# Batch 1's time shift mix goes to VectorE, wv is loaded in four pieces, five more zero matmuls and new orders

## The chip, the cores and the metric

The kernel runs on one core of one Trainium2 chip. The metric is the device time of one execution in microseconds (us). The engines are TensorE (PE in the profile, PEld for its weight loads), VectorE (DVE), ScalarE (ACT), GpSimd (POOL) and SyncE (SP); the last two issue most of the transfers, and ScalarE a few.

## The reference

Two layers, the second fed by the first. Everything comes and goes in float32.

```python
# attention, 8 batches x 8 heads, 576 positions, 64 wide
q_s = softmax(q, axis=-1)
k_s = softmax(k, axis=2)                       # over the positions
kv  = einsum('bhsd,bhse->bhde', k_s, v)
x   = einsum('bhsd,bhde->bhse', q_s, kv)       # then laid out as (8, 576, 512)
# channel mix
x_prev = x shifted by one position, zeros first
xk = mu_k * x + (1 - mu_k) * x_prev            # 512 wide
xr = mu_r * x + (1 - mu_r) * x_prev
k  = relu(xk @ w_k)                            # 512 x 1024
v  = (k * k) @ w_v                             # 1024 x 512
out = sigmoid(xr @ w_r) * v                    # w_r is 512 x 512
```

## The kernel before, in words

**Two halves of the work.** The attention goes by pairs (b, g): batch b, and g is 0 or 1 for half of the heads. The channel mix goes by ten units of up to 512 positions (`UNITS`, two halves of four batches each); a unit covers positions of one or two batches.

**Names.** Every step is an operation with a name, put on one engine (function `graph`). ORDER is a long string of those names, and it alone sets in which sequence each engine gets its steps; a number behind a colon is the buffer that the step takes. An engine works strictly through its own list, so a step that waits holds up everything behind it on that engine. For pair bg:

- `load{bg}{q,k,v}{n}` fetches the raw tiles (batches 0 and 1 in two parts of 288 KB, later ones as one of 576 KB), L204; `expq`, `expk` (L328) and `cast` for v (L334) are ScalarE's; `rsum`, `rrec`, `scale` normalise q on VectorE (L343, L347, L352).
- `TKV{bg}` is one block on TensorE: it turns q (L367) and forms k-softmax times v (L397). `rz` and `w` (L404, L414) bring the result back on VectorE as the small matrix of the attention, `qt` (L375) copies the turned q back on ScalarE.
- `X{bg}` forms x. Where the mix is **not folded** (batches 2 to 7) it is one block of 8 matmuls (L537), done inside the next pair's block, then called `B{bg}`, or alone for the pairs in ALONE. ScalarE copies x out (`xs`, `xb`, L543 and L546), and VectorE makes the mix: `edge`, `diff` (x minus shifted x, L555), four `sc` (times mu, L560), and two `mix` (plus shifted x, L565), `mix{bg}0` for xk and `mix{bg}1` for xr.
- Where it is **folded** (FUSED: batches 0 and 1) the small matrix is first multiplied by mu and by 1 - mu (`kvn`, L414 for batch 1; `wp{bg}0` on VectorE and `wp{bg}1`, for batch 1 on GpSimd, L475). Then `X{bg}0` and `X{bg}1` give xk and xr straight from TensorE, 16 matmuls each (L487), and `x{bg}{m}0` (ScalarE) and `x{bg}{m}1` (VectorE) copy them out (L497).

A unit i has `k{i}{f}` (eight, L621; a trailing .2 is the second half of one that was split by g), `relu{i}{f}` on ScalarE (L608), `sq{i}{f}` on VectorE (L612), `r{i}{m}` with w_r (L653), `th{i}{m}` on ScalarE (L658), `v{i}{m}{h}` with w_v (L673, h counts its parts), `o{i}{m}` on VectorE (L679) and `st` for the store. In unit 0 a v goes in as many parts as w_v has pieces, and a part waits for its piece alone; in the other units it has two parts.

**The ramp.** The q and k of batch 0 come through the queues of SP and ScalarE. Everything else is issued by GpSimd in the order that ORDER gives: v of batch 0, the weights `wk00`, `wk01`, `wk10`, `wk11` (quarters of w_k, tiles wk_aa to wk_bb), `wr`, `wv0` to `wv2`, `muload` (mu, that only the unfolded mix needs) and batches 1 to 7. At most eight of GpSimd's transfers are under way: the ninth issue waits until the first has landed, and so on. That makes GpSimd's own waits a record of landings. `k` steps that need g=0 alone want wk_aa, their .2 parts wk_ab; `k04` to `k07` want both wk_ba and wk_bb. Before there is real work, TensorE does matmuls on a tile of zeros (`fill`, L294), 22 of them.

Of the kernel before, what the change touches and what calls it, by code (L numbers as in the profile page):

```python
# [44 lines left out]
ACT!load00q0:0 zero ident load00q1 ACT!load00k0:1 load01q1:2 ACT!load01q0 rows load00v consts warm  # L45
load00k1 load01v late load01k0:3 load10q0:4 wk00 wk01 expq001:0 expq000 load11q0:5 rsum001:0
ACT!load01k1 rsum000 load10k0:6 expq011:1 rrec001 wk11 rrec000 rsum011:1 fill:1 fill.2:2 fill.3:3
fill.4:0 fill.5:1 fill.6:2 fill.7:3 fill.8:0 fill.9:1 fill.10:2 fill.11:3 fill.12:0 fill.13:1
fill.14:2 fill.15:3 fill.16:0 wide:0 scale000:0 expq010 expk000:0 rsum010 expk001 scale001
widecopy wk10 rrec010 fill.17:1 fill.18:2 KV001:0 rrec011 scale010:1 KV000 T00:1 rest Z00 qt00:0  # L50
scale011 rz00:0 expk010:1 fill.19:3 fill.20:1 fill.21:1 T01:3 edge00 kvn00:0 load10q1 expk011
fill.22:1 KV010:2 wp000:0 expq100:2 wr wp001 X000:1.0 qt01:1 KV011 x0001 Z01 load10k1 x0000 rz01:1
X001:0.3 kvn01:1 wp010:1 k02:0 x0010 edge01 k00:1 x0011 X010:1.0 load11q1 k03:2 x0100 x0101 k01:3
wv0 rsum100:2 k00.2 expk100:2 load10v1:7 k02.2 wp011 expq110:0 k03.2 relu00:0 k01.2 load10v0
X011:0.1 relu01:1 k07:1 sq01:0 load11v0:8 sq00 expq101 k05:3 load11v1 relu02:2 rsum101 relu03:1
k06:0 rrec100 sq02 relu05:0 sq03 x0110 k04:2 x0111 relu06:2 sq05 load11k1:9 r00:3 relu07:1
# [6 lines left out]
X110:1.0 mucopy k13:3 load30v0:8 x1101 x1100 k11:0 wp101 o01 expq210:2 k13.2 rsum200:0 k11.2
load31k0:9 relu13:1 X111:0.1 relu11:0 load40q0:10 k12:2 x1111 x1110 k17:3 o03 expk200:1 load30k0:0
sq11:1 k10:0 st03.2 sq13 k16:1 st00 expq300:0 rrec200 rsum210:1 load40v0:2 st03 X101:1.0 st01
relu17:2 k12.2 x1011 st00.2 x1010 k10.2 load31v0:3 sq17 relu16:0 k14:3 scale200:1 relu10:1
relu12:2 r12:1 cast210:0 sq10 load60q0:1 TKV20:0 rsum300:2 relu14:1 r11:0 th12:4 rrec210 rrec300
load41q0:4 rz20:1 expk210:2 k15:2 sq12 w20:0 scale210:2 r10:3 qt20:1 v120:1 sq16 relu15:2
scale300:0 expq310:1 B21:1.0 load50q0:5 sq14 th10:5 v110:2 rz21:2 sq15 xs20:0 xb20 w21:1
load40k0:7 rsum310:3 v100:3 qt21:0 v121 edge20 diff20:0 th11:6 v111 cast300:1 sc2000:0 X21:0.1  # L70
sc2011:1 o11 r13:0 xs21:1 load41k0:8 xb21 sc2010 o12 v101 expk300:0 edge21 rrec310 r20:2 diff21:1
expk310:1 load41v0:0 sc2001 v130:1 sc2101:2 mix200 th20:1 load60v0:9 TKV30:1 sc2100 th13:0
sc2111:0 mix210 v131 cast310:2 sc2110 k27:2 cast400:0 o13 load51q0:3 rz30:0 k21:0 scale310:1
st13.2 relu27:0 load50k0:2 st13 expq400:2 k22:1 o10 k20:2 w30:2 relu22:1 load71v0:10 st10 mix201
qt30:2 st11 k23:3 sq27:0 st11.2 rsum400:0 relu21:2 k24:1 st01.2 relu23:0 st10.2 B31:0.1 mix211
expk400:2 sq23 k26:0 rz31:1 relu24:0 rrec400 load50v0:7 sq21 xb30:0 w31:0 k25:3 sq24 scale400:2
relu20:2 r22:1 xs30 qt31:1 sq20 r23:2 edge30 diff30:0 relu25:0 B40:1.0 relu26:2 sq22 sc3001:2
expq410:0 v200:3 sc3000 mix300 th22:0 v220:0 load71k0:4 rz40:2 sq25 th23:6 rsum410:1 xs31:1 r21:1
xb31 v230:2 sq26 expq500:1 edge31 sc3011:1 v201 diff31:1 cast410:1 load61q0:5 w40:1 v231 sc3101:0
sc3100 th21:3 rrec410 load61k0:0 mix310 v221 expq510:2 o23 r30:1 o20 qt40:0 load71q0:3 k33:2  # L80
# [6 lines left out]
rrec600 st23.2 sc4001:0 th33:2 scale510:2 v331 expq610:1 k46:3 sc4000 qt51:0 relu43:0 o33
load60k0:5 B50:1.0 relu46:1 cast510:0 scale600:0 k47:2 st23 k42:0 cast600:1 v300:3 load70k0:1 sq46
qt60:2 sq44 rz50:1 mix400 v311 relu47:1 xs41:1 xb41 v320:2 o31 relu42:2 sq47 v301 expq700:2 st31.2
edge41 sq42 diff41:1 st21 r41:1 st21.2 expk510:2 o30 v321 sc4101:1 st30.2 sc4100 sq43 st31 k45:0  # L90
sc4110:2 mix410 st30 r40:3 relu45:1 expk600:0 o32 v410:0 sq45 rsum610:1 th41:6 k50:2 sc4111 k52:1
relu50:2 w50:0 rsum700:2 cast610:2 v411 k51:2 relu52:0 o41 mix411 k53:1 relu51:1 rrec610 B51:0.1
# [18 lines left out]
relu81:2 st73.2 sq80:0 k83:2 sq81 relu82:0 k84:1 sq82 relu83:1 k85:0 sq83 relu84:2 k86:3 sq84
relu85:0 k87:2 sq85 relu86:1 r80:1 sq86 relu87:2 r81:0 sq87 th80:5 v800:3 th81:4 v810:2 v801 v811
o80 r82:1 st80 o81 st80.2 r83:0 th82:6 st81 st81.2 v820:3 th83:0 v830:2 v821 v831 o82 k90:1 st82
o83 k91:0 st82.2 relu90:0 k92:3 st83 relu91:1 sq90:1 k93:2 relu92:2 sq91 st83.2 k94:1 relu93:0
sq92 k95:0 relu94:1 sq93 k96:3 relu95:2 sq94 k97:2 relu96:0 sq95 r90:1 relu97:1 sq96 sq97 r91:0
th90:3 v900:3 th91:2 v901 v910:2 o90 v911 st90.2 st90 v910.2:1 o91 v911.2 st91.2 st91 o91.2 st91.3
# [734 lines left out]
```

## Time and profile before

The three timed executions took 195.57, 195.60 and 195.91 us, median 195.6. The profiled execution took 195.56 us; its span, from the first to the last instruction, is 193.8 us, so 1.8 us lie around it.

| what | profiled execution |
|---|---|
| its time, and its span | 195.56 us, 193.8 us |
| granted TensorE clock, mean | 0.997 |
| VectorE busy | 149.7 us, 77% |
| ScalarE busy | 140.8 us, 73% |
| last matmul ends, read from TensorE's timeline | 190.1 us |

To read it: busy shares are means over a ramp, a long middle and an end that have different limits. The timeline of an engine lists its instructions with their start, what they took and, in brackets, how long the engine stood before them and who ended that.

### The profile page before, as it was taken

To read this page: it belongs to the slowest core of one execution; us is meant where nothing else is said; L and a number is where in the kernel's file an instruction comes from. 1 tells how busy PE (TensorE), PEld (TensorE's weight loads), DVE (VectorE), ACT (ScalarE), POOL (GpSimd) and SP (SyncE) were. 2 spreads that over 40 slices of the span, in tenths; PEclk is the share of its full clock that TensorE was granted. 3 is DMA by queue.
4 is the path that set the end of the run, shared out by engine and by line. 5 is a ranking of instruction groups with operands and counts; after the bars stand their busy time and mean duration, and the time that the engine had idled before them with its cause. 6 is when DMAs were issued, how large, how long until landed. Compare 5 with 4: busy or idle time off the path is not lost.

```text
span 193.8 us, 4763 instructions
## 1 busy us (share of the span) xinstructions
PE 186.3 (96%) x1873; PEld 90.4 (47%) x1873; DVE 149.7 (77%) x347; ACT 140.8 (73%) x218; POOL 43.5 (22%) x70
## 2 busy tenths in 40 slices
PE   7789999999999999999999999999999999999992
PEld 2264445435444554554555444444444444444751
DVE  1977668699999999999989998999925469622532
ACT  3777899899999999989996798767325732652340
POOL 8444347794324212341110000000000000000000
PEclk9999999999999999999999999999999999999998
DMA  6999999999999999899799604787334122403413
GB/s 198 315 267 292 268 347 303 401 390 392 414 391 391 392 408 355 258 331 351 169 220 113 223 4 96 156 207 150 70 71 92 57 50 58 112 0 80 96 42 108
DMA packets 23586, 41.86 MB, mean 216 GB/s; under 512 B 9344, under 2 KB 12684, under 8 KB 23564
## 3 DMA queue, kind: packets, MB, share of 16 engines
q0 software_dynamic: 9440, 27.99, 46.1%
q1 hardware_dynamic: 13308, 12.13, 24.8%
q10 hardware_dynamic: 816, 1.44, 2.1%
...
## 4 chain that ended last, share of the span: by engine, by line
PE 81%; DMA 12%; POOL 3%; ACT 2%; issue 0%; DVE 0%; POOLq 0%
PE mm_c L673 11%; PE mm_d L673 10%; PE mm_c L621 8%; PE mm_a L621 7%; PE mm_b L621 7%; PE mm_b L653 7%; PE mm_d L621 7%; DMA wk_bb<-in_moe_w_k_dram 7%; PE mm_a L673 6%; DMA raw_h<-in_v_dram 5%; PE mm_b L673 5%; PE mm_a L653 4%; PE mm_d L653 3%; PE mm_c L653 1%; PE att_b L397 1%; PE att_a L537 1%
## 5 line engine op out<-in xcount | busy, mean ns | idle before, releaser
L673 PEld LDWEIGHTS <-k_a 128*128 128x128 bf16 x144 | 13.8, 98 | 16.7 <-issue 0.5
L653 PEld LDWEIGHTS <-xr 128*128 128x128 bf16 x144 | 13.9, 98 | 16.2 <-issue 0.2
L673 PEld LDWEIGHTS <-k_b 128*128 128x128 bf16 x152 | 14.4, 98 | 15.0 <-issue 0.2
L653 PE MATMUL mm_b<-wr,xr 128*128 128x512 bf16 x64 | 16.4, 379 | 0.0
L621 PEld LDWEIGHTS <-wk_ab 128*128 128x128 bf16 x80 | 7.6, 98 | 8.2 <-issue 0.8
L621 PEld LDWEIGHTS <-wk_bb 128*128 128x128 bf16 x80 | 7.8, 98 | 7.7
L621 PEld LDWEIGHTS <-wk_aa 128*128 128x128 bf16 x80 | 7.4, 98 | 8.2 <-issue 0.9
L621 PEld LDWEIGHTS <-wk_ba 128*128 128x128 bf16 x80 | 7.5, 98 | 7.8 <-issue 0.2
L653 PE MATMUL mm_a<-wr,xr 128*128 128x512 bf16 x36 | 9.3, 380 | 0.0
L673 PE MATMUL mm_c<-wv_a,k_a 128*128 128x512 bf16 x32 | 8.2, 379 | 0.0
L608 ACT ACTIVATE rel_b<-mm_b 128x512 bf16<-128x512 f32 (+1 forms) x7 | 4.0, 571 | 4.9 <-PE mm_b L621 4.8
L608 ACT ACTIVATE rel_a<-mm_b 128x512 bf16<-128x512 f32 (+1 forms) x8 | 4.6, 572 | 4.0 <-PE mm_b L621 3.6
L621 PE MATMUL mm_c<-xk,wk_aa 128*128 128x512 bf16 (+1 forms) x26 | 7.3, 363 | 0.0
L621 PE MATMUL mm_c<-xk,wk_ab 128*128 128x512 bf16 (+1 forms) x26 | 7.3, 363 | 0.0
L612 DVE TENSOR_TENSOR k_a<-rel_b 128x512 bf16<-128x512 bf16 (+1 forms) x14 | 5.3, 380 | 2.5 <-ACT rel_b L608 2.5
L673 PE MATMUL mm_d<-wv_a,k_b 128*128 128x512 bf16 x28 | 7.2, 379 | 0.0
L653 PE MATMUL mm_d<-wr,xr 128*128 128x512 bf16 x28 | 7.2, 379 | 0.0
L612 DVE TENSOR_TENSOR k_b<-rel_a 128x512 bf16<-128x512 bf16 (+1 forms) x14 | 5.5, 390 | 1.8 <-ACT rel_a L608 1.3
L608 ACT ACTIVATE rel_c<-mm_a 128x512 bf16<-128x512 f32 (+1 forms) x11 | 6.0, 549 | 0.7 <-PE mm_a L621 0.7
L612 DVE TENSOR_TENSOR k_b<-rel_b 128x512 bf16<-128x512 bf16 (+1 forms) x14 | 5.5, 390 | 1.3 <-ACT rel_b L608 0.9
L612 DVE TENSOR_TENSOR k_b<-rel_c 128x512 bf16<-128x512 bf16 (+1 forms) x12 | 4.7, 391 | 1.9 <-ACT rel_c L608 1.6
L621 PE MATMUL mm_d<-xk,wk_ba 128*128 128x512 bf16 (+1 forms) x22 | 6.1, 360 | 0.0
(352 smaller groups left out, 534.0 us busy)
## 6 DMA issues: line engine op xcount, KB each, us to landing
...
```

The costliest lines, as they stand in the source:

```text
L397: kn.nc.tensor.matmul(kn.half(slot, r)[two[u], KVO:KVO + n], lhsT=kn.eks[ek.index][two[r], j, u, :], rhs=by, start=(j == 0), stop=(j == J ...
L537: kn.nc.tensor.matmul(kn.half(slot, u)[two[r], to:to + n], lhsT=kn.ws[w.index][two[u], r, :], rhs=x_columns(r, u, at, n), start=True, stop ...
L608: kn.nc.scalar.activation(out=kn.rels[rel.index][:, 0:n], in_=kn.bank(kf)[:, 0:n], func=ACT.Relu, scale=HALF_ROOT)
L612: kn.nc.vector.tensor_tensor(out=kn.k2s[k2.index][:, fc, 0:n], in0=kn.rels[rel.index][:, 0:n], in1=kn.rels[rel.index][:, 0:n], op=ALU.mult)
L621: kn.nc.tensor.matmul(kn.bank(kf)[:, 0:n], lhsT=kn.wk[fc // 4][ct % 2][:, ct // 2, (fc % 4) * 128: (fc % 4) * 128 + 128], rhs=kn.xs[0][:, ...
L653: kn.nc.tensor.matmul(kn.bank(rps), lhsT=kn.xs[1][:, ct, c:c + 128], rhs=kn.wr[:, ct, :], start=(ct == 0), stop=(ct == CT - 1))
L673: kn.nc.tensor.matmul(kn.bank(vps)[:, 0:width], lhsT=kn.k2s[k2.index][:, ft, 128 * m:128 * m + 128], rhs=wv_of(ft)[:, part], start=(ft == ...
```

## The change

- FUSED names pairs now and holds only those of batch 0. So for batch 1 `kvn`, `wp`, the four folded X blocks and the eight `x` copies go. Pair (1, 0)'s X is done inside (1, 1)'s block, which is now called `B11`; `X11` is alone; each pair has `w`, `xs`, `xb`, `edge`, `diff`, four `sc` and two `mix`.
- w_v comes in four pieces of two row tiles each rather than in three of 4, 2 and 2; unit 0's v steps have four parts.
- `muload` goes from GpSimd's queue to SP's, behind SP's loads of batch 0.
- FILLS goes from 22 to 27; the five are placed behind `fill.18`, right before `KV001`, the first real block.
- ORDER is new throughout. (Below, q100 is `load10q0`, the first part of pair (1, 0)'s q, and so on.) In GpSimd's queue the q, k and v of batch 1 go ahead of wv, and partly of the other weights. Behind batch 0's v it was q100, wk00, wk01, q110, k100, wk11, wk10, q101, wr, k101, q111, wv0, v101, v100, v110, v111, k111, k110, wv1, wv2, v20, mu. It is wk00, q110, q101, q100, wk01, q111, wk11, wk10, k101, v101, k100, v100, wr, v111, k111, k110, v110, wv0, wv1, wv2, wv3, q21, v20. On TensorE `TKV10` is ahead of unit 0's r steps, `B11` behind them and ahead of all of unit 0's v steps, and half of unit 4's k steps go in front of and between unit 3's. VectorE and ScalarE follow.

```diff
-WV = (0, 4, 6, 8)
+WV = (0, 2, 4, 6, 8)
-FILLS = 22
+FILLS = 27
-FUSED = (0, 1)
+FUSED = ((0, 0), (0, 1))
-ALONE = ((2, 1), (B - 1, 1))
+ALONE = ((1, 1), (2, 1), (B - 1, 1))
...
-th02:2 scale101:2 v020:3 wv2 scale100 cast101:0 v030:1 load20v0:10 rrec111 cast100 scale111:0
-muload v000:0 th01:3 rsum110 cast110:1 v010:2 load20q0:0 rrec110 cast111 scale110 TKV10:0
+relu06:0 load11v0 k05:3 relu05:2 wv0 wv1 rrec111 scale111:0 TKV10:0 sq07 wv2 rz10:2 r01:0
+relu04:1 r03:2 r02:3 w10:0 r00:1 qt10:2 cast111:1 expk111:0 wv3 expk110 cast110 sq04 load21q0:10
+scale110 th01:0 B11:1.0 th00:1 v010:0 rz11:0 sq05 load20v0:0 sq06 th03:2 v030:1 v000:2 xb10:0
+xs10 w11:1 edge10 v001 qt11:0 v031 v011 diff10:0 sc1001:0 sc1010:1 X11:0.1 sc1000 sc1011 v002
...
-            kn.nc.gpsimd.dma_start(out=kn.mu_sb[4 * m:4 * m + 4, :], in_=bass.AP(
+            kn.nc.sync.dma_start(out=kn.mu_sb[4 * m:4 * m + 4, :], in_=bass.AP(
...
-    mu_load = add("POOL", emit_mu_load, name="muload")
+    mu_load = add("SP", emit_mu_load, name="muload")
...
-        fused = b in FUSED
+        fused = (b, g) in FUSED
...
-        i = max(i for i in range(3) if WV[i] <= ft)
+        i = max(i for i in range(len(WV) - 1) if WV[i] <= ft)
```

More of the change, by code (lines that the diff above doesn't have):

```diff
@@ L44 @@
 ORDER = """
[L45 to L56, printed above, removed]
@@ L63 @@
[L63 to L74, printed above, removed]
@@ L75 @@
[L75 to L80, printed above, removed]
@@ L87 @@
[L87 to L92, printed above, removed]
@@ L111 @@
[L111 to L116, printed above, removed]
+ACT!load00q0:0 zero ident load00q1 ACT!load00k0:1 load01q1:2 ACT!load01q0 rows load00v consts
@@ new lines @@
+warm load00k1 load01v late load01k0:3 wk00 load11q0:4 load10q1:5 expq001:0 expq000 load10q0
+rsum001:0 ACT!load01k1 rsum000 wk01 expq011:1 rrec001 load11q1 rrec000 rsum011:1 fill:1 fill.2:2
+fill.3:3 fill.4:0 fill.5:1 fill.6:2 fill.7:3 fill.8:0 fill.9:1 fill.10:2 fill.11:3 fill.12:0
+fill.13:1 fill.14:2 fill.15:3 fill.16:0 muload wide:0 scale000:0 expq010 expk000:0 rsum010
+expk001 scale001 widecopy wk11 rrec010 fill.17:1 fill.18:2 fill.23:3 fill.24:1 fill.25:2 fill.26:3 fill.27:1 KV001:0 rrec011 scale010:1 KV000
@@ new lines @@
+T00:1 rest Z00 qt00:0 scale011 rz00:0 expk010:1 fill.19:3 fill.20:1 fill.21:1 T01:3 expk011
+kvn00:0 wk10 fill.22:0 mu:1 edge00 wp000:0 mucopy load10k1:6 qt01:1 X000:1.0 KV010:2 KV011 Z01
+wp001 x0001 edge01 x0000 expq110:2 load10v1:7 X001:0.3 load10k0 x0010 expq101:0 rz01:1 kvn01:1
+wp010:1 expq100 x0011 wp011 k03:0 X010:1.0 load10v0 k00:1 k02:2 x0101 rsum100:2 rrec100 k01:3
+rsum101 x0100 scale100:2 k02.2 k03.2 k00.2 relu03:0 sq03:0 expq111 relu00:1 wr k01.2 rsum110:3
+relu02:2 X011:0.1 rrec101 relu01:0 sq00 scale101 sq01 rrec110 k07:0 sq02 x0111 load11v1:8
@@ new lines @@
+rsum111 k04:1 x0110 expk101:2 cast101:0 expk100 cast100 relu07:1 k06:2 load11k1:9 load11k0
+relu06:0 load11v0 k05:3 relu05:2 wv0 wv1 rrec111 scale111:0 TKV10:0 sq07 wv2 rz10:2 r01:0
+relu04:1 r03:2 r02:3 w10:0 r00:1 qt10:2 cast111:1 expk111:0 wv3 expk110 cast110 sq04 load21q0:10
+scale110 th01:0 B11:1.0 th00:1 v010:0 rz11:0 sq05 load20v0:0 sq06 th03:2 v030:1 v000:2 xb10:0
+xs10 w11:1 edge10 v001 qt11:0 v031 v011 diff10:0 sc1001:0 sc1010:1 X11:0.1 sc1000 sc1011 v002
+th02:3 load30q0:2 v012 mix100 xs11:1 v020:3 xb11 edge11 v003 v021 v022 load20q0:1 v013 v032 v023
@@ new lines @@
+diff11:1 o00 sc1101:2 sc1100 o01 k12:2 v033 expq210:1 mix110 load20k0:3 sc1111:0 o03 k11:0 k11.2
+cast200:2 mix101 sc1110 k12.2 k13:1 load21k0:5 load21v0:4 load31q0:6 k13.2 expq300:0 relu11:1
+sq11:1 load31k0:7 st01.2 load30k0:9 st03.2 o02 mix111 st00 k10:0 k10.2 k14:3 expq200:2 rsum200:0
+relu12:2 rrec200 relu13:0 r11:2 expk200:1 st02 relu10:1 sq12 load40v0:8 th11:4 k17:1 k16:0 sq13
+expk210:2 scale200:1 r12:2 relu14:2 TKV20:1 relu16:0 rsum210:1 sq10 cast210:0 k15:3 rz20:1
+load30v0:10 rrec210 w20:2 relu17:1 th12:5 v110:0 r10:1 sq16 scale210:2 rsum300:2 load61v0:0
@@ new lines @@
+relu15:0 r13:2 qt20:1 sq15 B21:0.1 expq310:2 rrec300 sq17 sq14 th10:6 v100:3 load40k0:2 rz21:2
+v111 load40q0:1 xs20:0 xb20 v120:1 st00.2 load31v0:3 w21:0 qt21:2 rsum310:3 edge20 st03 st02.2
+expk300:0 rrec310 o11 X21:1.0 diff20:0 r20:0 v101 xb21:1 scale300:0 xs21 cast300:1 v121 edge21
+diff21:1 sc2000:2 TKV30:1 sc2001 load50v0:5 th20:1 load41q0:4 expk310:1 th13:2 load51q0:6
+sc2101:1 sc2100 v130:0 v131 mix200 expk400:2 load71v0:9 mix210 o12 k21:2 o13 o10 cast400:2
+rz30:0 k23:1 st11 sc2011:0 w30:1 cast310:0 relu23:0 sc2110:2 load50q0:10 scale310:1 k27:0 k22:3
@@ new lines @@
+sc2010 k20:1 relu21:1 load60v0:7 st11.2 st10 sc2111 k25:2 relu27:2 sq27:0 mix211 mix201 qt30:0
+expq400:1 relu22:2 B31:0.1 xs30:1 k24:0 sq21 rsum400:0 relu20:1 sq20 rz31:1 xb30 rrec400 st13
+st01 k26:3 w31:2 r30:1 relu24:1 qt31:1 load50k0:2 load41v0:8 r22:0 scale400:2 sq23 edge30 sq22
+th30:3 relu25:0 diff30:0 B40:1.0 sq24 sc3000:1 r21:1 rz40:2 relu26:2 xb31:0 sq25 xs31 v220:2
+r23:3 sq26 st13.2 edge31 diff31:1 th22:4 sc3001 sc3100:2 sc3101 mix300 v200:0 v221 th21:0
+cast500:1 mix310 o22 th23:2 expq410:0 expq500:2 v201 sc3110:0 sc3111 o20 k47:1 expq510:1 k33:3
@@ new lines @@
+load41k0:3 load60q0:1 rsum410:1 rrec410 k43:2 k30:0 load61q0:5 relu33:1 sc3010:1 st20 relu30:0
+sq33:1 relu47:2 relu43:1 v210:3 st12 k46:0 w40:0 k42:1 v211 qt40:2 cast410:0 expk410:0 sq30
+v230:2 v231 scale410:0 o21 rsum500:2 relu42:0 cast600:2 load61k0:4 k37:3 o23 sq43:0 rrec500
+relu37:1 sq42 sq47 sc3011 mix311 st22.2 k41:1 mix301 st10.2 k34:2 k40:3 B41:0.1 expk500:1
+relu40:0 st23 k31:3 st23.2 relu34:2 sq40 xs40:0 st20.2 xb40 rz41:0 sq34 r40:2 relu41:0 k36:1
+sq37 relu31:2 k32:3 w41:1 scale500:1 th40:6 load71k0:10 r32:2 load70q0:6 relu46:1 qt41:0 sq31
@@ new lines @@
+scale600:0 st33 v401 mix411 mix410 edge50 o40 qt60:0 diff50:1 cast610:1 r41:1 v410:3 v411
+B60:1.0 st31 rsum700:1 sc5001:0 expk710:2 st40.2 st33.2 rrec700 th41:5 xs51:1 k53:2 k50:1 k57:0
+xb51 relu50:0 relu53:2 edge51 st21 sq50:0 diff51:0 relu57:1 r50:1 k54:2 sq57 rz60:0 expq710:1
+st30.2 v320:0 o41 w60:1 relu54:0 sc5101:2 k51:2 sc5100 expq610:0 sq54 sc5111:1 v321 mix510
+th50:4 relu51:1 o32 st32.2 r51:3 rsum610:2 k55:1 sc5000 th51:0 k52:2 k56:0 cast710:0 r52:3
+sc5010:2 mix500 rrec610 sq53 expk610:0 sc5110 st31.2 sc5011 scale610:1 relu55:0 relu52:2 th52:3
@@ new lines @@
+cast700:2 B61:0.1 qt61:1 sq52 k65:1 sq51 mix501 sq55 rsum710:3 k66:2 relu66:2 k61:3 v520:2
+relu56:1 xs60:0 relu65:0 xb60 sq56 r53:0 scale700:2 v521 th53:1 o52 mix511 relu61:1 rz61:1
+edge60 k62:1 v510:0 w61:2 sq61:1 r60:3 B70:1.0 relu62:1 rrec710 diff60:0 xb61:1 v511 v530:2 sq62
+st41 rz70:2 sq66 k67:1 xs61 relu67:1 w70:0 st32 scale710:0 v531 sc6011:0 st40 o51 k63:0 edge61
+diff61:1 sc6101:2 sc6110:1 th60:2 sc6111 k60:1 sc6100 relu60:2 mix611 sc6010 qt70:2 sq65
+sc6000:1 sq60 sc6001 o53 qt71:0 relu63:0 mix600 mix610 r62:3 k64:1 B71:0.1 v500:0 rz71:0 v501
@@ new lines @@
+o50 sq67 st53 th62:6 mix601 xb70:1 k73:3 xs70 k76:2 sq63 relu73:2 sq73:0 k77:0 relu76:1 sq76
+k70:3 w71:1 edge70 diff70:1 X71:1.0 relu77:0 v620:2 relu64:2 sc7000:1 sc7010:2 xb71:0 xs71
+st41.2 relu70:1 sq64 edge71 v600:0 sq77 v621 st51.2 o62 diff71:0 sc7001 r63:1 st52 st53.2 th63:5
+k75:3 k71:2 relu75:2 relu71:0 v601 sq71 sc7101:0 mix700 k72:1 sc7100 st52.2 o60 relu72:0 st60.2
+sc7111:1 sq70 k74:3 st60 mix710 r72:2 th72:1 r71:1 k83:0 v630:2 v631 sq72 sc7011 o63 th71:3
+relu74:1 k85:1 r61:3 th61:2 v610:2 relu83:0 v611 o61 st50 st61 sq74 st62 k81:3 relu81:1 r70:0
@@ new lines @@
+k82:2 sq75 sq83:1 k86:3 relu82:2 sq82 relu86:0 k84:2 th70:2 sq81 sc7110 k80:3 relu80:2 relu85:1
+st63 sq80 st63.2 v700:0 sq86 v701 r80:3 o70 k87:1 relu84:2 th80:6 relu87:0 sq84 sq85 mix701
+v720:2 r73:0 v721 sq87 o72 st72.2 mix711 st70.2 v730:3 v800:1 v801 r81:2 v731 st51 o80 th73:5
+r82:0 st50.2 st80 th81:0 v810:1 v811 o73 st73 st73.2 st72 o81 v710:2 v711 o71 st70 st71.2 st71
+st80.2 r83:3 th82:4 st81 st81.2 v820:0 th83:5 v830:1 v821 v831 o82 k90:2 st82 o83 k91:3 st82.2
+relu90:2 k92:0 st83 relu91:1 sq90:0 k93:1 relu92:0 sq91 st83.2 k94:2 relu93:2 sq92 k95:3
@@ L117 @@
+relu94:1 sq93 k96:0 relu95:0 sq94 k97:1 relu96:2 sq95 r90:2 relu97:1 sq96 sq97 r91:3 th90:1
+v900:0 th91:2 v901 v910:1 o90 v911 st90.2 st90 v910.2:2 o91 v911.2 st91.2 st91 o91.2 st91.3
 st91.4
@@ L695, in unit @@
                     o = add("PE", lambda v=v_part, a=a, e=e: v(range(a, e)),
-                             squares[a:e] + [o or r] + [wv_done[i] for i in range(3)
+                             squares[a:e] + [o or r] + [wv_done[i] for i in range(len(WV) - 1)
                                                         if WV[i] < e and WV[i + 1] > a],
@@ L802 @@
     kn.wv = [const.tile([128, e - a, C], BF16, name=f"wv_{x}")
-             for x, a, e in zip("abc", WV, WV[1:])]
+             for x, a, e in zip("abcd", WV, WV[1:])]
     kn.wr = const.tile([128, CT, C], BF16, name="wr")
```

34 lines of the change are left out of this document (6 added, 28 removed).

## The prediction, on record before the result

> **What bounds the kernel now.** I read the page's first two parts, then busy time by stage, then the timelines of GpSimd, TensorE and VectorE in the ramp.
>
> ```profile
> PE 186.3 (96%) x1873; PEld 90.4 (47%) x1873; DVE 149.7 (77%) x347; ACT 140.8 (73%) x218; POOL 43.5 (22%) x70
> PE   7789999999999999999999999999999999999992
> DVE  1977668699999999999989998999925469622532
> ```
> ```profile
> 16.00:40.00 24.00, 23.69 (x260) 10.69 (x258) 17.04 (x43) 20.52 (x33) 14.88 (x24) 1.00 1.12 321
> 40.00:78.00 38.00, 38.00 (x534) 18.24 (x533) 37.15 (x78) 37.38 (x54) 14.13 (x22) 1.00 1.01 387
> 78.00:140.00 62.00, 62.00 (x581) 30.48 (x580) 59.73 (x131) 50.06 (x77) 5.75 (x8) 1.00 0.75 183
> 140.00:190.00 50.00, 50.00 (x303) 24.82 (x300) 24.93 (x56) 22.02 (x40) 0.00 (x0) 1.00 0.27 64
> ```
>
> The second fence gives busy us of PE, PEld, DVE, ACT and POOL in four stretches, then granted clock (full), DMA share and GB/s. TensorE is without a hole from 16 us on: its work is the bound. But from 40 to 78 us VectorE and ScalarE stand only 0.85 and 0.6 of 38 us, so three engines are bounds together there. VectorE has room before it (7.0 us idle from 16 to 40) and after 140. So work taken from TensorE pays only if VectorE fits its new work into the idle time of the ramp.
>
> What makes it idle there is the loads. GpSimd's timeline shows their landings, as each issue waits for the transfer eight places ahead:
>
> ```profile
> 12.13 0.57 POOL L204 DMA_DIRECT2D raw_e<-in_q_dram  x1 [1.98 <-DMA vb_b<-in_v_dram]
> 14.15 0.55 POOL L204 DMA_DIRECT2D raw_g<-in_k_dram  x1 [0.54 <-DMA wk_aa<-in_moe_w_k_dram]
> 16.41 0.55 POOL L204 DMA_DIRECT2D raw_f<-in_q_dram  x1 [1.71 <-DMA wk_ab<-in_moe_w_k_dram]
> 19.04 0.54 POOL L204 DMA_DIRECT2D raw_h<-in_v_dram  x1 [0.65 <-DMA wk_bb<-in_moe_w_k_dram]
> 20.28 0.54 POOL L204 DMA_DIRECT2D raw_i<-in_v_dram  x1 [0.70 <-DMA wk_ba<-in_moe_w_k_dram]
> 23.59 0.54 POOL L204 DMA_DIRECT2D raw_j<-in_k_dram  x1 [2.04 <-DMA wr<-in_moe_w_r_dram]
> ```
>
> A landing lies 0.29 us ahead of the issue: wk_bb 18.75, wk_ba 19.99 (1.24 for a quarter of w_k), wr 23.3. The two issues of raw_i at 20.28 and 21.00 land after 9.6 us each, so a 288 KB piece takes 0.72. The queue is a conveyor; what counts is the place in it. VectorE's two longest waits of the ramp follow from it, and one folded X block on TensorE is seen between its neighbours:
>
> ```profile
> 20.81 0.42 DVE L612 TENSOR_TENSOR k_a<-rel_b 128x512 bf16<-128x512 bf16 x1 [1.64 <-ACT rel_b L608]
> 25.95 0.76 DVE L343 TENSOR_REDUCE rsum_d<-eq_a 128x9 f32<-128x576 bf16 x1 [1.98 <-ACT eq_a L328]
> ```
> ```profile
> 35.91 0.44 PE L487 MATMUL att_a<-qt_c,wp_a 64*64 64x288 bf16 x8
> 36.18 0.42 PE L487 MATMUL att_b<-qt_c,wp_a 64*64 64x288 bf16 x8
> 36.53 0.60 PE L673 MATMUL mm_d<-wv_c,k_a 128*128 128x512 bf16 x2
> ```
>
> **The change part by part.**
>
> *TensorE's work.* A folded X of batch 1 goes from 35.91 to 36.53, 0.62 us (the last fence); four are 2.48. In come X11 alone (X21's start to the next, 0.37) and X10 inside B11, which makes that block 0.95 instead of TKV11's 0.78. The mu matmul (0.15) moves to the ramp. The same matmuls of unit 0's v in four parts instead of three: 0.04. Sum -1.9 us.
>
> *Five fills.* At 0.22 us each (starts 5.04 to 5.25) 1.1 us, between fill.18's end at 8.19 and KV001 at 9.58, which waits 1.39 us for ScalarE. Nothing; without that wait they would cost 1.1.
>
> *mu on SP.* SP's last load lands at 12.08, issued 4.66, 7.4 us; two of 2 KB behind it land at about 12.4, and TensorE is at that place at 12.1. The matmul then stands ahead of X000 (13.11 before, held by VectorE until 12.7) and KV010; I take nothing, at most 0.5 us if they land at 13. GpSimd loses two issues and two products of 0.87, which nobody waited for.
>
> *The start of unit 0.* On ScalarE expq100 no longer stands ahead of qt01, so k03 starts about 0.6 us before the old k02 (15.59). That is lost again: k07 needs wk_ba, one 288 KB piece later in the queue, 20.7, where k07 was at 20.69. Four k steps of 0.865 bring 24.2, TKV10 then waits for cast100 until 24.4 and ends 25.2.
>
> *wr, then B11.* wr stands behind four more pieces than before: 23.3 + 4 x 0.72 = 26.2. TensorE waits 1.0 us and does four r steps until 29.7. v110 lands four pieces behind wr, 29.1; with its cast (0.67) 29.85, and ScalarE's own list comes to the same time. B11 then ends at 30.85, where the old TKV11 ended at 33.22. wv in four pieces lands from 30.3 to 34.1, each ahead of its v steps; the fourth transfer hides in a queue of seven. If it did not, one 1.24 piece late would be 1.2.
>
> *TensorE from there to the end.* From 33.22 to the last matmul's end, 190.13, are 156.9 us. Behind B11 stand also the first halves of v (3.46) and X11 (0.37), and not the four X (2.48) and mu: +1.0 with hand-overs. Alone, TensorE would end at 30.85 + 157.9 = 188.8, 1.4 earlier.
>
> *VectorE.* Per pair it loses two copies (0.68 from start to start), wp (0.41) and kvn (0.26), and gains diff (0.68), four sc (0.28), two mix (0.67) and w (0.20): +1.3, for both +2.6 us. ScalarE is even: two copies of 0.52 against xb 0.90 and xs 0.15. Behind B11 I follow VectorE's list. ScalarE has three th ahead, so xb10 and xs10 end at 32.4; edge, diff, four sc, mix100 until 35.0; X11's copy is there at 35.2; edge, diff, o00, two sc, o01, mix110 until 38.45, and k11.2 wants it at 39.1. o03 waits 0.5 for its matmuls. From x1101 (39.22) to mix310 (77.91) VectorE took 38.7 us; the new list holds 1.4 less between mix110 and mix310 (rsum410, two copies and small ones are elsewhere, mix101 and mix111 are in). So mix310 ends at 38.45 + 38.7 - 1.4 + 0.5 = 76.3. TensorE alone would be at the first step that needs it, k47, at 76.1. ScalarE needs qt31 for B40 some 0.4 us ahead of TensorE.
>
> *The sum.* k47 starts at 76.4. The old one, k33, started at 79.07, with 111.06 us to the last matmul; behind k47 stand v230 and v231 as well (1.73). End 76.4 + 112.8 = 189.2, 0.95 us earlier. After 78 us VectorE's margins in the new list are all above 1 us, and the end of the kernel keeps its steps. 195.56 - 0.95 = **194.6 us**, the profiled execution being 0.04 below the median.
>
> *A rule against it.* Issues of GpSimd at 58.94 and 59.99, with sc running beside them, took 0.72 us, as the one at 42.58 without. The Trainium skill (SBUF — State Buffer, SBUF: two separate sides) has a VectorE operation in a two-port mode lock GpSimd out, which then can't write descriptors, so its transfers starve. The trace does not bear it out for sc.
>
> **The rivals.**
>
> - *VectorE fills no idle time.* If it stands before mix310 as long as now (7.0 of 16 to 40 and 0.85 after), its 0.7 us more work up to there puts mix310 at 78.6; k47 78.7, the end 191.5, **196.9 us**. It turns slower once mix310 ends after 77.2, 0.9 later than I have it. For it: most of that idle is waits for ScalarE and loads (3.6 of 7.0 in two waits, rsum111 and sq01). Against: batch 1's q now lands before 18.3, so rsum110, scale101 and rsum111 fill exactly those waits.
> - *The loads come sooner and nothing waits.* Between wk_aa and wk_ab there are 2.26 us for one quarter where 1.24 is usual; without that hole wr lands at 25.2, B11 ends at 30.3, bound by ScalarE, mix310 follows: **193.9 us**. With every wait gone from k07 on B11 ends at 29.4 and TensorE's own path gives **193.1**.
> - *Nothing comes of it:* loads or VectorE later by just what TensorE saves, **195.5 us**.
> - *GpSimd locked out.* Eight sc of 0.36 hold its issues of batches 2 and 3 up by 2.9 us; the copies and exponentials behind them come that late less some 0.5 of slack: **197.0 us**. That is the time by the rule above.
>
> **How the numbers follow.** Forecast (194.2 to 195.1) 0.44, sooner 0.21, nothing 0.13, VectorE 0.19, GpSimd 0.03. Range 193.3 to 196.6, which leaves out a little of the first rival and the lower end of the second. A change of 0.2%, 0.4 us, is about what can be told from none: faster 0.65, within 0.13, slower 0.22. Faster cases alone span 193.1 to 195.1.
>
> **What would show it.** In the changed kernel's trace: no fill next to a longer wait for KV001; the mu matmul before 13; wr's landing at 26.2 and a wait of about 1 us before the first r; B11's end near 30.85; k47 near 76.4 with mix310 just ahead; VectorE idle 16 to 40 well under 7. I am wrong if wr lands after 27.5, if mix310 ends after 77.2, or if TensorE shows waits after 80 us.

## The result: 3.5% slower, and nearly all of it in one place

The changed kernel took 202.96 us (median of four, 201.96 to 203.12) where the kernel before took 195.75 beside it: ratio 1.035, interval 1.0327 to 1.0373. Forecast were 194.6 us and a range of 193.3 to 196.6. The profiled execution of the changed kernel took 203.02 us, with a span of 201.2.

The first two parts of its page, the lines that answer to those shown of before, and the granted clock (line numbers are two higher than before, L623 for L621):

```profile
PE 188.6 (94%) x1830; PEld 90.9 (45%) x1830; DVE 151.5 (75%) x353; ACT 139.0 (69%) x218; POOL 41.3 (21%) x65
PE   7899879999999999999999999999999928999991
DVE  1899936999999999988999999999772403442531
PEclk9999999999999999999999999999999995999998
```

TensorE was 9 or more in every slice from the ramp to the last one before. Now slice 33 (161 to 166 us) is a 2, and in slice 34 the clock is half. Busy time by stage (us of PE, PEld, DVE, ACT, POOL, then clock, DMA share, GB/s) says the same:

```profile
16.00:40.00 24.00, 22.24 (x235) 10.16 (x231) 18.67 (x46) 21.13 (x35) 14.35 (x22) 1.00 1.13 321
40.00:78.00 38.00, 38.00 (x510) 18.43 (x509) 37.57 (x80) 37.41 (x54) 12.82 (x19) 1.00 1.00 382
78.00:140.00 62.00, 61.79 (x618) 30.15 (x617) 59.77 (x133) 49.83 (x78) 5.68 (x8) 1.00 0.64 176
157.80:172.00 14.20, 9.76 (x34) 3.78 (x33) 4.56 (x12) 4.01 (x8) 0.00 (x0) 0.76 0.20 55
```

From 158 to 172 us TensorE is busy for 9.76 of 14.2 us only, at a clock of 0.76 on average, and the other engines for less than 5. Rows of the timelines of SP, ScalarE and TensorE there tell how:

```profile
157.82 0.59 SPq L709 DMA_DIRECT2D out_dram<-th_c  x1
158.46 0.52 SPq L709 DMA_DIRECT2D out_dram<-th_g  x1
159.03 4.02 SPq L691 DMA_DIRECT2D out_dram<-th_f  x2
```
```profile
160.50 0.60 ACT L610 ACTIVATE rel_a<-mm_d 128x512 bf16<-128x512 f32 x1 [0.27 <-PE mm_d L623]
165.99 0.60 ACT L660 ACTIVATE th_c<-mm_a 128x512 f32<-128x512 f32 x1 [4.89 <-DMA out_dram<-th_c]
```
```profile
161.60 0.59 PE L623 MATMUL mm_d<-xk,wk_ab 128*128 128x512 bf16 x2
166.64 1.01 PE L675 MATMUL mm_a<-wv_a,k_a 128*128 128x512 bf16 x2 [4.44 <-ACT th_c L660]
168.29 1.06 PE L675 MATMUL mm_a<-wv_c,k_a 128*128 128x512 bf16 x2
170.00 1.91 PE L655 MATMUL mm_d<-wr,xr 128*128 128x512 bf16 x4
171.71 0.70 PE L623 MATMUL mm_b<-xk,wk_ba 128*128 128x512 bf16 x2
172.68 0.59 PE L675 MATMUL mm_c<-wv_a,k_a 128*128 128x512 bf16 x2
```

L709 is a store that the kernel before has too: for row tiles 1 and 2 of unit 6 (MERGED) one transfer writes all 128 tokens, 256 KB, instead of two of 64. Its target has two output rows as the outermost dimension. In the new ORDER `r61` and what hangs on it stand late, so `st61` is issued at 157.82 and `st62` behind it. The gate `th70` on ScalarE is to write the same buffer, th_c, and waits until 165.99. Three relus stand behind it on ScalarE, and those four operations are to free all four mm banks. TensorE has none left after 162.19 and stands for 4.44 us. Then four steps (`v700`, `v701`, `r80`, `k87`) go at half clock, the last of them in part: 6.04 us from 166.64 to 172.68, where four of 0.865 are 3.46. Together 4.44 + 2.58 = 7.02 us; the last matmul ends at 197.08, against 190.13 before.

The kernel before issues its merged stores at 141.63 and 145.59, and the buffer of the first is next written at 171.98, 30 us later. Here it is wanted 3 us later. SP and ScalarE of the kernel before:

```profile
141.63 0.59 SPq L707 DMA_DIRECT2D out_dram<-th_f  x1
145.59 0.52 SPq L707 DMA_DIRECT2D out_dram<-th_e  x1
171.98 0.60 ACT L658 ACTIVATE th_f<-mm_b 128x512 f32<-128x512 f32 x1 [0.27 <-PE mm_b L653]
```

The ramp, where the change was made, came out much as forecast. TensorE's two waits and `k47`, then VectorE's wait for `B11` and GpSimd's issues that show the landings:

```profile
21.32 0.60 PE L623 MATMUL mm_a<-xk,wk_ba 128*128 128x512 bf16 x2 [0.57 <-DMA wk_ba<-in_moe_w_k_dram]
26.77 1.04 PE L655 MATMUL mm_a<-wr,xr 128*128 128x512 bf16 x4 [1.04 <-DMA wr<-in_moe_w_r_dram]
76.65 0.38 PE L623 MATMUL mm_b<-xk,wk_ba 128*128 128x256 bf16 x2
```
```profile
31.61 0.17 DVE L406 RECIPROCAL rz_a<-att_b 128x2 f32<-128x2 f32 x1 [3.52 <-PE att_b L399]
32.86 0.29 DVE L416 TENSOR_TENSOR w_b<-att_b,rz_a 128x128 bf16<-128x128 f32 x1 [0.43 <-ACT xb_a L548]
```
```profile
21.56 0.54 POOL L206 DMA_DIRECT2D raw_j<-in_k_dram  x1 [0.75 <-DMA wk_ba<-in_moe_w_k_dram]
27.01 0.71 POOL L304 DMA_DIRECT2D wv_d<-in_moe_w_v_dram  x1 [1.54 <-DMA wr<-in_moe_w_r_dram]
```

So two questions were left: is it the merged store, and why is the rest only level with the kernel before and not 0.95 us faster?

### The profile page after: what moved, and what is told of

Its sections match the earlier page's. It is cut to its first block, busy times and chain, and to the rows that moved or that the text cites. A ratio compares the mean times of both kernels' runs of the same rounds, so it can differ in the third digit from the quotient of the medians.

```text
span 201.2 us, 4642 instructions
## 1 busy us (share of the span) xinstructions
PE 188.6 (94%) x1830; PEld 90.9 (45%) x1830; DVE 151.5 (75%) x353; ACT 139.0 (69%) x218; POOL 41.3 (21%) x65
## 4 chain that ended last, share of the span: by engine, by line
PE 66%; DMA 14%; DVE 8%; ACT 7%; issue 2%; POOL 2%; DVEq 0%; POOLq 0%; ACTq 0%
PE mm_a L675 10%; PE mm_c L675 9%; PE mm_b L623 7%; DMA raw_f<-in_q_dram 6%; PE mm_a L623 5%; PE mm_d L623 5%; PE mm_c L623 5%; PE mm_b L675 4%; PE mm_d L655 4%; DMA out_dram<-th_c 4%; DMA raw_g<-in_k_dram 4%; PE mm_d L675 3%; PE mm_b L655 3%; PE mm_c L655 3%; PE mm_a L655 2%
## 5 line engine op out<-in xcount | busy, mean ns | idle before, releaser
L623 PEld LDWEIGHTS <-wk_ab 128*128 128x128 bf16 x80 | 7.8, 98 | 8.0 <-DMA wk_ab<-in_moe_w_k_dram 0.3
L623 PEld LDWEIGHTS <-wk_bb 128*128 128x128 bf16 x80 | 7.8, 98 | 7.8 <-issue 0.2
L623 PEld LDWEIGHTS <-wk_ba 128*128 128x128 bf16 x80 | 7.5, 99 | 8.3 <-DMA wk_ba<-in_moe_w_k_dram 0.9
L623 PEld LDWEIGHTS <-wk_aa 128*128 128x128 bf16 x80 | 7.5, 98 | 8.2 <-issue 1.0
L655 PE MATMUL mm_c<-wr,xr 128*128 128x512 bf16 x40 | 10.3, 379 | 0.0
L614 DVE TENSOR_TENSOR k_b<-rel_c 128x512 bf16<-128x512 bf16 x11 | 4.5, 412 | 7.3 <-ACT rel_c L610 7.3
L655 PE MATMUL mm_b<-wr,xr 128*128 128x512 bf16 x36 | 9.2, 379 | 0.0
L675 PE MATMUL mm_a<-wv_a,k_a 128*128 128x512 bf16 x14 | 4.6, 414 | 4.4 <-ACT th_c L660 4.4
L610 ACT ACTIVATE rel_c<-mm_c 128x512 bf16<-128x512 f32 (+1 forms) x9 | 5.2, 575 | 4.9 <-PE mm_c L623 4.9
L614 DVE TENSOR_TENSOR k_a<-rel_a 128x512 bf16<-128x512 bf16 (+1 forms) x16 | 6.0, 375 | 1.9 <-ACT rel_a L610 1.6
L623 PE MATMUL mm_b<-xk,wk_ba 128*128 128x512 bf16 (+1 forms) x24 | 6.8, 366 | 0.0
L623 PE MATMUL mm_d<-xk,wk_aa 128*128 128x512 bf16 (+1 forms) x24 | 6.7, 362 | 0.0
L623 PE MATMUL mm_d<-xk,wk_ab 128*128 128x512 bf16 (+1 forms) x24 | 6.7, 361 | 0.0
L623 PE MATMUL mm_b<-xk,wk_bb 128*128 128x512 bf16 (+1 forms) x24 | 6.7, 361 | 0.0
```

The lines of the kernel that those rows point to most:

```text
L610: kn.nc.scalar.activation(out=kn.rels[rel.index][:, 0:n], in_=kn.bank(kf)[:, 0:n], func=ACT.Relu, scale=HALF_ROOT)
L614: kn.nc.vector.tensor_tensor(out=kn.k2s[k2.index][:, fc, 0:n], in0=kn.rels[rel.index][:, 0:n], in1=kn.rels[rel.index][:, 0:n], op=ALU.mult)
L623: kn.nc.tensor.matmul(kn.bank(kf)[:, 0:n], lhsT=kn.wk[fc // 4][ct % 2][:, ct // 2, (fc % 4) * 128: (fc % 4) * 128 + 128], rhs=kn.xs[0][:, ...
L655: kn.nc.tensor.matmul(kn.bank(rps), lhsT=kn.xs[1][:, ct, c:c + 128], rhs=kn.wr[:, ct, :], start=(ct == 0), stop=(ct == CT - 1))
L675: kn.nc.tensor.matmul(kn.bank(vps)[:, 0:width], lhsT=kn.k2s[k2.index][:, ft, 128 * m:128 * m + 128], rhs=wv_of(ft)[:, part], start=(ft == ...
```

## The experiments

### First: what makes the stall

**The stores apart** (label unmerged).

```diff
-MERGED = ((6, 1), (6, 2))
+MERGED = ()
-... o61 st50 st61 sq74 st62 k81:3 ...
+... o61 st50 st61 st61.2 sq74 st62 st62.2 k81:3 ...
```

> The changed kernel with the stores of rows m=1 and m=2 of unit 6 as two stores of 64 rows each instead of one of 256 KB. Theory: the merged store st61 holds th_c for 8.1 us (157.82 to 165.95) because the two-row outer dimension of its target spreads it over 2 of the 16 DMA engines only; the gate th70 waits for that buffer, the four mm banks behind it stay full, and TensorE stands 4.44 us and then runs four steps at half clock (6.04 us instead of 4 x 0.865, +2.58). Two plain stores land 2.4 us after their issue, th70 comes at about 161.1, both parts of the loss go: 202.96 - 4.44 - 2.58 = 195.9 us, level with the kernel before. Rival 1: the place of r61, o61 and its store so late in the order is the cause, whatever form the store has; then th70 stays within 1 us of 166 and the time within 202 to 203.5. Rival 2: the loss is VectorE's added mix work or the later loads, and the wait for th_c only shows it; then the wait goes elsewhere and the time stays above 201.

Measured: 195.69 us, ratio to before 1.0000 (0.9992 to 1.0009). The place of `r61` is untouched, so its lateness alone does not make the stall. ScalarE and TensorE of this kernel at the same place:

```profile
160.59 0.60 ACT L610 ACTIVATE rel_a<-mm_d 128x512 bf16<-128x512 f32 x1 [0.27 <-PE mm_d L623]
161.09 0.59 ACT L660 ACTIVATE th_c<-mm_a 128x512 f32<-128x512 f32 x1
```
```profile
161.69 0.59 PE L623 MATMUL mm_d<-xk,wk_ab 128*128 128x512 bf16 x2
162.12 0.59 PE L675 MATMUL mm_a<-wv_a,k_a 128*128 128x512 bf16 x2
```

`th70` follows its relu with no wait, at 161.09 as expected. Why the one form is slow is seen in the DMA share, the last but one number of busy time by stage; the first line is the changed kernel while `st61` runs by itself, the second the unmerged one:

```profile
159.50:162.50 3.00, 2.69 (x13) 1.11 (x12) 1.04 (x3) 1.19 (x2) 0.00 (x0) 1.00 0.13 31
```
```profile
158.00:161.50 3.50, 3.50 (x18) 1.59 (x17) 1.93 (x6) 2.10 (x4) 0.00 (x0) 1.00 0.63 146
```

0.13 of 16 engines is two engines, at 31 GB/s; the same rows as plain stores get 146. The form was as slow in the kernel before: from 143 to 145.5 us, beside its first merged store, the share is 0.13 too, at 29 GB/s. Most of the trace's packets of 2 KB take 84 ns, and 64 of them on each of two engines are 5.4 us. Some 1.2 us pass before the first starts, and packets at the beginning and beside `st63` take longer: 8.1 us from issue to landing. The Trainium skill (DMA: Bandwidth & Descriptors, Why a DMA increments its semaphore by 16 and not by 1) has the number of engines follow from the slowest dimension of both sides that isn't one: the largest number up to 16 that divides both sizes. Sides of 128 and 2 make that two, and the trace agrees. A single transfer with the 64 tokens outermost was not tried.

**Two buffers more** (th_two_more). The merged stores stay; `th70` and `th80` get buffers of their own, in the v tiles of batch 0.

```diff
-    kn.ths = buffers("th", [128, C], F32)
+    kn.ths = buffers("th", [128, C], F32) + [
+        v[:].rearrange("p u c -> p (u c)").bitcast(F32)[:, 0:C] for v in kn.vbs]
-... th70:2 ... th80:6 ...
+... th70:7 ... th80:8 ...
```

> The changed kernel with two more th buffers, laid over the v tiles of batch 0 that nobody reads any more: th70 writes the one, th80 the other. The merged stores stay. Theory (a buffer held by a slow store): th70 follows its relu at about 161.1, th80 is free too, the time is 195.9 us, and st61 still takes about 8 us to land with nobody waiting for it; th73 needs th_f, whose stores land at about 171.4, and is wanted at 171.9, so up to 0.5 us may be lost there. Rival (the stores themselves cost, through the queue or the memory): the time stays above 198 although nothing waits for th_c.

Measured: 195.87 us, 1.0008 (0.9999 to 1.0017). The slow stores cost next to nothing when nobody waits for the buffer. `th73` did wait for th_f until 172.02, against 171.9 wanted. The plain stores of `st63` behind the merged ones are late too: the first landed 12.4 us after its issue, where such a store takes 2.4 in the unmerged kernel.

**One buffer more** (th_one_more): the same, but `th80:6` is left on th_g.

```diff
-... th70:2 ... th80:6 ...
+... th70:7 ... th80:6 ...
```

> The same with one more buffer only, for th70; th80 still writes th_g, which the second merged store st62 reads. Theory: both merged stores go through the same 2 engines one after the other, so st62 lands at about 171.3 wherever th70 is; th80 waits for it, holds mm_d, and v730, wanted at 168.25, starts at about 171.95: a stall of 3.7 us in another place, 199.6 us if the clock stays full, up to 202.2 if it drops to half for four steps again. Rival (only the one wait for th_c costs): 195.9 us, as with two buffers.

Measured: 201.55 us in one execution. TensorE of this kernel:

```profile
168.04 0.59 PE L675 MATMUL mm_c<-wv_d,k_a 128*128 128x512 bf16 x2
172.23 1.01 PE L675 MATMUL mm_d<-wv_a,k_a 128*128 128x512 bf16 x2 [3.59 <-ACT th_g L660]
173.03 1.06 PE L675 MATMUL mm_d<-wv_b,k_a 128*128 128x512 bf16 x2
```

The stall moved to the next merged store: `v730` at 172.23 after 3.59 us, forecast 171.95 after 3.7, and the steps behind it slow until 175.5. So the mechanism is a buffer held by a store, and both merged stores hold theirs.

**Zero matmuls in the stall** (busy_stall): 16 of them between `k80` and `v700`.

```diff
+    for i in range(16):
+        slot = Slot("att")
+        def warm_fill(slot=slot):
+            return kn.nc.tensor.matmul(kn.half(slot, 0)[:, 0:512], lhsT=kn.still[:, 0:128], ...)
+        add("PE", warm_fill, [zero], [slot], [slot], name="fillw")
-... st63.2 v700:0 ...
+... st63.2 fillw:0 fillw.2:0 ... fillw.16:0 v700:0 ...
```

> The changed kernel with 16 zero matmuls of 512 columns (about 0.22 us each, 3.5 us) between k80 and v700 on TensorE, into an att bank that nobody uses any more; the wait for th_c stays. Theory (the half clock follows from TensorE standing idle): v700 starts at 166.6 as before, at full clock, its four steps take 3.46 us instead of 6.04: 202.96 - 2.58 = 200.4 us. Rival (the half clock comes from something else, as the load of the chip at that time): it stays half and the time is 202.5 to 203.5.

Measured: 200.53 us, 1.0251 (1.0233 to 1.0269).

```profile
161.99 3.62 PE L305 MATMUL att_a<-still 128*128 128x512 bf16 x16
166.62 0.59 PE L684 MATMUL mm_a<-wv_a,k_a 128*128 128x512 bf16 x2 [1.02 <-ACT th_c L669]
168.34 1.03 PE L664 MATMUL mm_d<-wr,xr 128*128 128x512 bf16 x4
```

`v700` starts where it did, but its two matmuls take 0.59 instead of 1.01. The clock falls because TensorE stands, and that is 2.4 of the 7.3 us. The Trainium skill (TensorE: Matmul & The Clock Gate, Part 1: The HAM clock gate) has the clock go to half after an idle window of about 3.4 us and come back after a busy one. The trace agrees: half after 4.44 and after 3.59 us of idle, not after 1.02. One number does not quite fit: in the first case the half clock begins 2.9 us after the modelled end of the last matmul, less than that window.

### Second: why the rest is not 0.95 us faster

All of these start from the unmerged kernel. A difference of 0.2% is about what they can tell: beside the next four, the kernel before scattered from 195.47 to 197.85, and two kernels with the same median of 195.67 got ratios of 1.0001 and 0.9982.

**Without the five fills** (no_fills).

```diff
-FILLS = 27
+FILLS = 22
-... fill.18:2 fill.23:3 fill.24:1 fill.25:2 fill.26:3 fill.27:1 KV001:0 ...
+... fill.18:2 KV001:0 ...
```

> The unmerged kernel without the five added zero matmuls ahead of KV001. Theory (they stand in TensorE's wait for ScalarE and cost and bring nothing): KV001 starts at 9.6 to 9.7 as with them, the gap ahead of it is 1.1 us longer, the time is 195.7 us within 0.2. Rival (they hold the clock or push KV001 back): the clock is lower than full after 9 us and the time above 196.2, or KV001 comes earlier and the time is below 195.4.

Measured: 195.67 us, 1.0001 (0.9974 to 1.0027). `KV001` starts at 9.68, after a wait of 1.57 us. The fills cost nothing and bring nothing.

**w_v in three pieces** (wv_three).

```diff
-WV = (0, 2, 4, 6, 8)
+WV = (0, 4, 6, 8)
-... wv3 ... v003 ... v013 ... v023 ... v033 ...
```

> The unmerged kernel with w_v loaded in three pieces of 4, 2 and 2 row blocks again, as the kernel before has it, and unit 0's v steps cut to match. Theory: the first piece is 2.5 us long and lands at about 32.05 instead of 30.8, v010 wants it at 31.5, so TensorE waits 0.55 us there: 196.2 us. Rival (hidden, since VectorE sets k47): 195.7 us.

Measured: 196.75 us, 1.0038 (1.0015 to 1.0060).

```profile
32.90 1.04 PE L674 MATMUL mm_a<-wv_a,k_a 128*128 128x512 bf16 x3 [0.54 <-DMA wv_a<-in_moe_w_v_dram]
```

The wait of 0.55 us is there, 0.54. In this execution most of the loads ahead of wv landed 0.5 to 0.8 us later than in the unmerged kernel (w_r at 27.54 for 26.74), so its own time, 197.65, is no measure; the ratio is, and 0.15 to 0.6% holds 0.55 us. The edit does a second thing, though: the three v steps ahead of `X11` are longer by two row tiles each, 1.3 us together, and `X11` starts at 36.89 for 34.38. So the ratio is the price of both, and the run does not part them.

**w_r in two halves** (wr_split).

```diff
-    wr_done = add("POOL", lambda: weight(kn.wr, kn.w_r, C, 0, 1, CT, 0), name="wr")
+    wr_done = [add("POOL", lambda i=i: weight(kn.wr[i], kn.w_r, C, 2 * i, 1, 2, 0), name="wr")
+               for i in range(2)]
-            r = add("PE", r_part, ... + [wr_done], [rps], [], name=f"r{index}{m}")
+            r = None
+            for cts in ((0, 1), (2, 3)) if index == 0 else ((0, 1, 2, 3),):
+                r = add("PE", lambda f=r_part, cts=cts: f(cts), ...
+                        + [wr_done[ct // 2] for ct in cts] + [r], [] if r else [rps], [], ...)
-... wr k01.2 ... r00:1 qt10:2 ...
+... wr wr.2 k01.2 ... r00:1 r01.2 r03.2 r02.2 r00.2 qt10:2 ...
```

> The unmerged kernel with w_r loaded in two halves of 1.2 us, and unit 0's four r steps cut in two: the first halves stand behind TKV10, the second halves behind them. It takes away the 1.1 us for which TensorE waits for w_r at 25.7. Theory (what was left of the forecast gain is held by the loads of the ramp): first halves from 25.7, second halves done at 29.2, B11 then waits for the cast of v110 at 30.3 and ends at 30.75, v010 finds wv's first piece at 30.8 instead of starting at 31.5; k47 0.7 earlier, 195.0 us. Rival 1 (VectorE, dense from 33 us to mix310, sets k47): it gets rz11 0.7 earlier as well, but ScalarE, dense until 32.8, gives xb10 no sooner: mix310 stays at 76.3, k47 at 76.7, 195.6 us. Rival 2: one more transfer in the queue of eight makes all later loads later: above 195.9.

Measured: 195.67 us, 0.9982 (0.9969 to 0.9996). The time is that of the first rival, 195.6. The wait for w_r is gone and TensorE is at unit 0's v steps 0.5 us sooner, but waits again behind them. TensorE, then VectorE, of this kernel:

```profile
30.49 0.48 PE L400 MATMUL att_b<-vv_b,ek_a 64*64 64x65 bf16 x36 [0.24 <-ACT vv_b L337]
34.51 0.22 PE L540 MATMUL att_b<-qt_a,w_b 64*64 64x64 bf16 x4 [0.66 <-ACT qt_a L378]
```
```profile
33.02 0.29 DVE L417 TENSOR_TENSOR w_b<-att_b,rz_a 128x128 bf16<-128x128 f32 x1 [1.16 <-ACT xb_a L549]
```

`X11` waits 0.66 us for `qt11` on ScalarE, and VectorE waits 1.16 for `xs10`, also ScalarE. `mix310` ends at 76.43. ScalarE was right behind TensorE all the time.

**More on VectorE** (vec_more): the eight products by mu of batch 1 done twice.

```diff
-                s = [add("DVE", lambda m=m, u=u: scale_x(m, u), [xdiff, mu_done],
+                s = [add("DVE", lambda m=m, u=u: [scale_x(m, u) for _ in range(2 if b == 1 else 1)],
+                         [xdiff, mu_done],
```

> The unmerged kernel with each of the eight products by mu of batch 1 (the sc operations, 0.28 us each) done twice on VectorE, 2.2 us more. Theory (VectorE is dense from 33 us to mix310, which is 0.4 us ahead of k47): mix310 ends 2.2 us later, k47 1.8 to 2.1 us later, 197.6 us. Rival (VectorE fills idle time of the ramp with it): mix310 moves by less than 0.5 us and the time is 195.7 to 196.0.

Measured: 199.26 us, 1.0164 (1.0144 to 1.0185): 3.5 us more, not 1.9.

```profile
39.62 1.54 DVE L562 TENSOR_SCALAR xm_c<-xd_b,mu 128x576 bf16<-128x576 bf16 x4
41.08 0.68 DVE L682 SCALAR_TENSOR_TENSOR th_a<-th_a,mm_a 128x512 f32<-128x512 f32 x1
```

Four in a row take 1.46 us from start to start of the next group, where the unmerged kernel's two take 0.56; the repeat onto the same output adds 0.45 each, not 0.28. `mix310` ends 3.6 us later, at 79.90, and TensorE comes to `k47` at 80.29, 3.6 later. VectorE, then, has no slack from `B11` to `mix310`: what is added there is paid in full.

**Less on VectorE** (vec_less): batch 1's mix without its products by mu, whose names also go from ORDER; part of the computation is left out.

```diff
+                if b == 1:
+                    o = add("DVE", lambda m=m: mix(m, kn.xds[xd.index]), ...)
+                    continue
```

> The unmerged kernel without the eight products by mu of batch 1, whose mix adds the bare difference: part of the computation is left out. VectorE does 2.2 to 2.9 us less. Theory (TensorE, without a hole from 26.8 us to k47, comes to k47 just when VectorE does): mix310 ends 2 to 3 us earlier, k47 stays at 76.6 to 76.7, 195.6 us. Rival (VectorE's added work is what took the forecast gain): k47 and the end come 0.5 us or more earlier, 195.2 or less.

Measured: 195.71 us, 0.9998 (0.9973 to 1.0022). `k47` starts at 76.70 as before. Taking the products from VectorE gives nothing: TensorE arrives at the same time by itself. `mix310`, however, ends at 76.31, not 2 to 3 us earlier. VectorE spent the time in waits for ScalarE and TensorE, 1.7 us of them at 36, 38 and 39.7 us. It has no slack there, but no lead to win either.

**The two casts of v11 to VectorE** (split_casts, on top of wr_split; casts_only, w_r in one piece). In ScalarE's list `th01` moves up, in between the two exponentials.

```diff
-            kn.nc.scalar.copy(
+            (kn.nc.vector.tensor_copy if (b, g) == (1, 1) else kn.nc.scalar.copy)(
-... qt10:2 cast111:1 expk111:0 wv3 expk110 cast110 sq04 load21q0:10 scale110 th01:0 B11:1.0 ...
+... qt10:2 expk111:0 wv3 th01:0 expk110 sq04 load21q0:10 scale110 cast111:1 cast110 B11:1.0 ...
```

> The kernel with w_r in two halves, and beside it the two casts of v11 (0.7 us each on ScalarE at 28 to 30.3) moved to VectorE, which stands idle from 28.3 to 31.0. Theory (after TensorE's wait for w_r is gone, ScalarE, dense from 19.3 to 33 us, holds xb10, xs10 and qt11, and with them VectorE's list and X11): th01 moves up to 28.5, xb10 starts when B11 ends at 30.7 to 31.0 instead of 31.7, X11's wait of 0.66 us goes, mix310 ends at 75.5, k47 starts at about 76.0; 195.0 us, ratio 0.9965. Rival 1 (VectorE's list behind it takes up the gain, or loads of batches 2 and 3 do): k47 stays at 76.7, 195.7 us. Rival 2 (the casts on VectorE hold GpSimd's descriptor writing): loads behind 28 us land later, 196 or more.

> The unmerged kernel with the two casts of v11 moved from ScalarE to VectorE alone, w_r still in one piece. Theory (two waits end at the same place, and taking away one leaves the other): TensorE still waits for w_r until 26.8 and is dense from there, so k47 stays at 76.7: 195.7 us, ratio 1.000. Rival (ScalarE alone was the bound): 195.0 us.

Measured: both parts together 195.28 us, 0.9973 (0.9956 to 0.9990); the casts alone 195.61 us, 0.9983 (0.9966 to 0.9999), too near to no change to be told from it by the bound above. ScalarE, then TensorE, with both:

```profile
30.62 1.02 ACT L546 CAST xb_a<-att_a 128x1024 bf16<-128x1024 f32 x1
```
```profile
33.34 0.22 PE L540 MATMUL att_b<-qt_a,w_b 64*64 64x64 bf16 x4
75.97 0.38 PE L624 MATMUL mm_b<-xk,wk_ba 128*128 128x256 bf16 x2
```

`xb10` is 1.1 us sooner, `X11` waits for nothing, and `k47` starts at 75.97, where 76.0 was expected. With the casts alone it starts at 76.46: TensorE still waits 1.08 us for w_r. Of the 0.7 us gained at `k47`, 0.5 are left at the last matmul (189.45 against 189.97). By its interval this version is 0.1 to 0.4% faster than the kernel before; the intervals of its two parts alone overlap with it, so that both are needed is read from `k47`, not from the times.

## Why the prediction was wrong, step by step

- *The step that failed* is the sentence "After 78 us VectorE's margins in the new list are all above 1 us, and the end of the kernel keeps its steps." The end keeps its work, but not its order, and the margin that broke is none of VectorE's. It is the chain from a store to a th buffer, from there to ScalarE's list and to TensorE's banks. The new ORDER has `st61` and `th70` on th_c so near to each other that the reuse comes 3 us after the issue. The lists were followed for the engines' work and not for the buffers' landings. Of the 8.4 us by which the forecast missed it cost 7.02 by the rows of the stall above and 7.3 by the unmerged run, and no rival held it. "TensorE shows waits after 80 us" was named as what would make the forecast wrong, without a place or a price.
- *TensorE's work, five fills.* Right: no difference without the fills.
- *mu on SP.* In the changed kernel the matmul ran at 12.66 and `X000` at 12.81, earlier than before (13.06). Nothing was lost; it was not tried by itself.
- *The start of unit 0, w_r.* Mechanism right, 0.6 us late: `k07` at 21.32 for 20.7, w_r's landing at 26.72 for 26.2, a wait of 1.04 for 1.0. The term that was mis-sized is the landing of wk_ba, which was put one piece of 0.72 behind the old one and came 1.3 behind it. `B11` ends at 31.5 for 30.85.
- *wv's fourth piece.* Right that it hides; with the three pieces of before TensorE waits 0.54 us here.
- *VectorE.* `mix310` ended at 76.29 in the unmerged kernel, forecast 76.3, and its +2.6 us fit. It stood 5.3 of the 24 us from 16 to 40, as forecast well under 7, and 3.5 of these are one wait, for `B11`. That this idle time gives no slack behind `B11` was not said: 3.6 us more cost 3.5. The rival "VectorE fills no idle time" did not come true.
- *The sum.* `k47` started at 76.65 for 76.4, set by TensorE and not, as forecast, by VectorE: TensorE has no wait ahead of it. From there to the last matmul, less the stall, are 113.4 us for 112.8; the unmerged kernel, which has no stall, took 113.3. Its matmuls are no slower: those of 512 columns lie 0.216 us apart from start to start in both kernels. What the sum put at nothing is a wait for `th41` ahead of `k50`, which makes 0.38 us from start to start, and three holes of 0.04 to 0.07 at 88.8, 107.2 and 131.2 us; that is the 0.5. The path of TensorE alone was short by as much: its terms (3.46 and 0.37 in, 2.48 and 0.15 out) make +1.2 and not +1.0, and from 31.50 to 189.97 the unmerged kernel took 158.5 us for 157.9.
- *The end.* So without the stall the last matmul ends at 189.97 for 189.2, and 0.16 us of the forecast gain of 0.95 is left there: 0.3 went up to `k47`, 0.5 behind it. The rest goes behind the last matmul, a stretch that the forecast took as unchanged. From its end to the end of the span are 3.65 us in the one trace of the kernel before and 3.91 to 4.15 in the twelve traces with the new ORDER, and so the unmerged kernel's ratio is 1.0000. Why the end is longer stays open.
- *The loads come sooner* did not come true either, and wr_split shows that it would have brought less than written: with TensorE's wait gone ScalarE is the next bound, at the same time.
- *GpSimd locked out.* Its issues beside `sc` still take 0.72 us, and casts on VectorE at 28 to 30 us moved no landing.
